# A fused dynamic convolution, LayerNorm and MLP on one core: W1 on SyncE's queue behind the first x, the first columns and their halo in one transfer, the first convolution chunk summed without VectorE, and a new order

## The chip, the cores and the metric

The kernel runs on one core of a Trainium2 chip. The metric is the device time of one execution in microseconds; the number that counts is the median of several runs.

## The reference

x has 8 batches of 4224 tokens of 192 channels, `weight_gen` has for each token 8 heads of 7 raw weights. What is computed, cut to its core:

```
w   = exp(weight_gen - max) / sum                # softmax over the 7 taps
y   = sum over k of w[.., k] * x[s - 6 + k]      # causal, 24 channels share a head's weight
xn  = (y - mean) / sqrt(var + 1e-6) * g          # over the 192 channels
out = y + relu(xn @ w1) @ w2                     # w1 192x768, w2 768x192, given as float64
```

## The kernel before

**Layout.** The 33792 tokens lie over the 128 partitions, 16 stretches of each of the 8 batches, so a partition owns C = 264 consecutive tokens, called columns. The convolution of a column reaches 6 columns back. Those of a stretch's first columns belong to the partition ahead (the halo); the first stretch of each batch has zeros there, written by a memset. x passes through a ring `X` of 36 columns with 6 halo columns ahead of it.

**Loops.** The columns are cut three ways: softmax parts (`SOFT`: 4, 8, then 12 columns), norm parts and convolution chunks. The norm parts are

```
PARTS = (4,) * 6 + (8,) * 6 + (12,) * 15 + (8, 4)
```

and a convolution chunk has at most 6 columns (4 at the start). TensorE works in 66 groups g0 to g65 of 4 columns, that is 512 tokens each; a 12-column part feeds three of them.

**The work of a chunk.** VectorE multiplies x by the weights for taps two at a time (L383, three products `pr` of two taps and one `y`). GpSimd issues two DMAs that add one half of a `pr` to its other half (L389), and then adds four `pr` halves into `y` (L386). For chunk 0 alone (`c < EARLY`, EARLY = 1) it is otherwise: one GpSimd addition of two whole `pr` (L399) and four additions by VectorE (L386). ScalarE then takes sums (L427) and squares (L432) of `y`, and a reciprocal root by logarithm and exponential (L455 to L457); VectorE refines it by a Newton step (L460 to L466); ScalarE writes the normalised `xh` (L478) and casts it to f16 `hl` (L485); GpSimd writes the low f16 part (L487); SyncE's queue moves it through a transposing DMA into `xT` (L491; two `hl` and three `xT` buffers).

**TensorE.** A group has three steps u0, u1, u2 of the first product (L506, 10 matmuls 128x512 each into `ph`). After each, ScalarE takes the relu into `hh` (L515), and VectorE the f16 remainder `hlo` (L517). The second product (L538 to L540) has four pieces of 18 matmuls, one for each column of a group; two of them stand between one step and another, so that they use `hh` and `hlo` of the group ahead. VectorE scales and adds it to `y` (L551), and a DMA takes `y` out (L558).

**Weights.** W1 and W2 come as pairs of 32-bit words. VectorE turns W1's words into f32 (L610 to L620, two row blocks of 128 and 64 rows, tiles `hh` for the words, `ph` and `hlo`), ScalarE takes sums of squares (L623), TensorE sums them over partitions (L630 and the matmul of L639, the first two matmuls of the program), VectorE makes a scale `c_gi` of them (L675), ScalarE scales W1 into `c_w1h` and keeps the scaled f32 (L680), GpSimd forms `c_w1l` (L683), and small DMAs shift row blocks (L686). W2 follows in the same way while the first groups run. W1's words are loaded by two DMAs on ScalarE's queue (L580), ahead of the two tiny loads of g. The loads of x (L287 halo, L290 and L292), of `weight_gen` (L298) and of W2 (L580) are on SyncE's queue.

**The order.** Nothing is scheduled by hand. Each operation is recorded with an engine, a cost and a due position `want`, in columns, which is the column that it works for less a number out of `WANT`, `W_WANT` or `FIRST`. `Plan.order` then places operations one by one on modelled engines: the earliest due of those that could start within `AHEAD` of the earliest, and that are due within `WINDOW` of the oldest operation left. The order so found is the program order of every engine's queue, and each engine keeps to it, waiting where an input or a buffer isn't ready.

Of the kernel before, what the change touches and what calls it, by code (L numbers as in the profile page):

```python
# [16 lines left out]
P = 128  # L17
# [2 lines left out]

PARTS = (4,) * 6 + (8,) * 6 + (12,) * 15 + (8, 4)
SOFT = (4, 8) + (12,) * 21
EARLY = 1
CHUNK = 6
RING = 36
HALF = 512
TINY = struct.unpack("<f", struct.pack("<I", (1023 - 126) << 20))[0]


WANT = {'load': 35.31, 'wload': 45.13, 'max': 23.73, 'sub': 26.8, 'exp': 29.21, 'sum': 19.41,  # L30
    'rcp': 16.76, 'inv': 19.08, 'mul': 14.75, 'conv': 17.87, 'step': 0.85, 'dma': -0.4, 'add':
    0.2, 'sums': 8.31, 'squares': 3.24, 'rstd': 5.29, 'newton': 6.27, 'xh': 1.75, 'lo': 6.1}
W_WANT = {'load': 23.7, 'a': 23.19, 'c': 24.61, 's1': 21.01, 'load2': 14.54, 'c2': 3.68, 's2':
    7.55}
FIRST = {'soft': -1.12, 'conv': -1.17, 'norm': 7.8}
AHEAD = 13.38
WINDOW = 11.37


class Buf:  # L40
# [11 lines left out]
class Plan:  # L52


    DMA_START = {"SP": 1250.0, "Pool": 650.0, "ACT": 1250.0}
    DMA_END = 1000.0

    def __init__(self):
# [30 lines left out]
    def order(self):  # L89
# [31 lines left out]
        while len(out) < len(self.ops):  # L121
            pick = None
            while by_want[lead].start is not None:
                lead += 1
            until = by_want[lead].want + WINDOW
            for e, c in cand.items():
                rows = [(t, o) for t, o in ((earliest(o), o) for o in c if o.want <= until)
                        if t is not None]
                if rows:
                    t0 = min(t for t, _ in rows) + AHEAD  # L130
                    row = min((r for r in rows if r[0] <= t0), key=lambda r: (r[1].want, r[1].rank))
# [25 lines left out]
def kernel(  # L157
# [10 lines left out]
    B, S, D = x.shape  # L168
# [3 lines left out]
    w1b, w2b = w1.bitcast(I32), w2.bitcast(I32)  # L172
    F = w1.shape[1]
    PAD = K - 1
    NF = F // P
    NB = 3
    C = B * S // P
    PB = P // B
# [4 lines left out]
    V, A, Q, T_, SY = nc.vector, nc.scalar, nc.gpsimd, nc.tensor, nc.sync  # L183
# [9 lines left out]
    X = cp.tile([P, PAD + RING, D], F32, name="x")  # L193
# [36 lines left out]
    def dma_ns(n):  # L230
        return n * P / 280.0
# [11 lines left out]
    xf = x.rearrange("b s d -> (b s) d")  # L243
# [26 lines left out]
    def xcol(t):  # L270

        return PAD + t % RING

    def xkey(t, back=False):
        return ("x", "h") if back else ("x", t % RING)

    def sp(want, fn, r, w, dma):
        op("SP", 450, want, fn, r=r, w=w, dma=dma)

    def load_x(ch):  # L280
        t0, n = ch["S"], ch["n"]
        want = t0 - WANT["load"]
        if t0 == 0:

            def first():
                src = bass.AP(tensor=xf.tensor, offset=(C - PAD) * D, ap=[[C * D, PB - 1], [PB * C * D, B], [1, PAD * D]])
                SY.dma_start(X[B:P, 0:PAD, :].rearrange("p t d -> p (t d)"), src)  # L287
            sp(want, first, [], [("x", "h")], dma_ns(PAD * D))
        elif t0 % RING == 0:
            sp(want, lambda: SY.dma_start(X[:, 0:PAD, :].rearrange("p t d -> p (t d)"), tokens(x, t0 - PAD, PAD)), [], [("x", "h")],  # L290
               dma_ns(PAD * D * 4))
        sp(want, lambda: SY.dma_start(X[:, xcol(t0) : xcol(t0) + n, :].rearrange("p t d -> p (t d)"), tokens(x, t0, n)), [],  # L292
           [xkey(t) for t in range(t0, t0 + n)], dma_ns(n * D * 4))

    def load_w(pa):
        t0, n = pa["S"], pa["n"]
        wb = pa["w"] = Buf("w")
        sp(t0 - WANT["wload"], lambda: SY.dma_start(at(wb)[:, :n, :].rearrange("p t f -> p (t f)"), tokens(wf, t0, n)), [], [wb],  # L298
           dma_ns(n * HK * 4))

    def early(s, what):
        return s - FIRST[what] * max(0.0, 1 - s / 12)

    def softmax(pa):
# [12 lines left out]
        def step(eng, cost, name, fn, r, w):  # L317
            op(eng, cost, S0 - WANT[name], fn, r, w)

# [31 lines left out]
    def conv(c):  # L351
        ch = chunks[c]
        t0, n, o = ch["S"], ch["n"], ch["so"]
        st = WANT["step"] * n / 6
        c0 = early(t0, "conv") - WANT["conv"]
        y = ch["y"] = Buf("y")
        prs = {k: Buf("pr") for k in (1, 3, 5)}
        wrap = t0 % RING == 0
        base = 0 if wrap else xcol(t0) - PAD
        xr = [xkey(t) for t in range(t0, t0 + n)]  # L360
        if wrap:
            xr.append(("x", "h"))
        else:
            xr += [xkey(t) for t in range(max(t0 - PAD, t0 // RING * RING), t0)]
            if t0 % RING < PAD:
                xr.append(("x", "h"))
        yw = [(y, j) for j in range(n)]

        def flat(k):
            if k == 0:  # L370
                return at(y)[:, :n, :].rearrange("p t d -> p (t d)")
            return at(prs[(k - 1) // 2 * 2 + 1])[:, (k - 1) % 2, :n, :].rearrange("p t d -> p (t d)")

        def mul(k, nk):
            wv = (WN[:, o * HK : (o + n) * HK].rearrange("p (m k) -> p k m", k=K)[:, k : k + nk, :]
                  .unsqueeze(3).broadcast_to([P, nk, n * H, G]))
            a = X[:, base + k : base + k + n, :]
            xv = bass.AP(tensor=a.tensor, offset=a.offset, ap=[a.ap[0], [D, nk], [G, n * H], [1, G]])
            if k:
                ov = at(prs[k])[:, :, :n, :].rearrange("p k t (h g) -> p k (t h) g", g=G)  # L380
            else:
                ov = at(y)[:, :n, :].rearrange("p t (h g) -> p (t h) g", g=G).unsqueeze(1)
            V.tensor_tensor(out=ov, in0=xv, in1=wv, op=ALU.mult)  # L383

        def add(k, E=Q):
            E.tensor_tensor(out=flat(0), in0=flat(0), in1=flat(k), op=ALU.add)  # L386

        def dma_add(to, k):
            Q.dma_start(flat(to), flat(k), accum_op=ALU.add, max_dma_last_dim=CHUNK * D * 4)  # L389

        nd = n * D
        for i, k in enumerate((1, 3, 0, 5)):
            op("V", v_ns(2 * nd if k else nd), c0 + 2 * i * st, lambda k=k: mul(k, 2 if k else 1),
               [*xr, "wn"], [(prs[k], 0), (prs[k], 1)] if k else yw)
        if c < EARLY:

            both = [(prs[k], h) for k in (1, 3) for h in (0, 1)]
            pp2 = [at_pair(prs[k], n) for k in (1, 3)]
            op("Pool", q_ns(2 * nd), c0, lambda: Q.tensor_tensor(out=pp2[0](), in0=pp2[0](), in1=pp2[1](), op=ALU.add),  # L399
               both[2:], both[:2])  # L400
            for i, (k, h) in enumerate(((5, 0), (5, 1), (1, 0), (1, 1))):
                op("V", v_ns(nd), c0 + (8 + i) * st, lambda k=k, h=h: add(k + h, V), [(prs[k], h)], yw)
            return
        for i, k in enumerate((1, 3)):
            op("Pool", 900, c0 + 2 * i * st + WANT["dma"], lambda k=k: dma_add(k, k + 1), [(prs[k], 1)],
               [(prs[k], 0)], dma=3300.0 * n / 6)
        for i, (k, h) in enumerate(((5, 0), (5, 1), (1, 0), (3, 0))):
            op("Pool", q_ns(nd), c0 + (4 + 2 * i) * st + WANT["add"], lambda k=k, h=h: add(k + h),
               [(prs[k], h)], yw)
# [161 lines left out]
    top, bot = slice(0, 64), slice(64, P)  # L571
    raw = (Buf("hh"), Buf("hh"), Buf("pr"))

    def words(i, o, n):
        return at(raw[i]).bitcast(I32).rearrange("p a b d -> p (a b d)" if i == 2 else "p j q -> p (j q)")[:, o : o + n]

    def load_weights():

        def dma(eng, E, want, dst, src, n, w):
            op(eng, 450, -W_WANT[want], lambda: E.dma_start(dst(), src), w=[w], dma=dma_ns(n))  # L580

        dma("ACT", A, "load", lambda: words(0, 0, 2 * F), w1b[0:P, :], 8 * F, raw[0])
        dma("ACT", A, "load", lambda: words(1, 0, 2 * F)[top, :], w1b[P:D, :], 4 * F, raw[1])
        dma("ACT", A, "load", lambda: W["g"][:, 0:1], gcol[0:P, :], 200, "g0")
        dma("ACT", A, "load", lambda: W["g"][top, 1:2], gcol[P:D, :], 100, "g1")
        wv2 = w2b.rearrange("(j p) d -> p j d", p=P)
        dma("SP", SY, "load2", lambda: words(2, 0, 2 * NF * D).rearrange("p (j d) -> p j d", d=2 * D), wv2,
            8 * NF * D, raw[2])

    def from_double(want, src, dst, n, sq, r, w, space="ph", rows=slice(0, P)):  # L590
# [14 lines left out]

        want = -W_WANT[want]
        op("ACT", a_ns(n), want, lambda: A.activation(mv(), part(1).bitcast(F32), AF.Square), r, [m])
# [17 lines left out]
    def w_scale(want, ss, bound, rt, r, w):  # L625


        pb = Buf("po")
        want = -W_WANT[want]
        op("PE", 240, want, lambda: T_.matmul(at(pb)[:, 0:1], ones, ss, start=True, stop=True), r, [pb],  # L630
# [18 lines left out]
    def weights():  # L649
# [5 lines left out]
        def f32(b, n, o=0):  # L655
            if b is not w2r:
# [5 lines left out]
                    [raw[1]], [wc], rows=top)  # L662
        want = -W_WANT["s1"]

# [35 lines left out]
        for h in range(3):  # L700
            from_double("c2", lambda h=h: words(2, 2 * h * tn, 2 * tn), lambda h=h: f32(w2r, tn, h * tn),
                        tn, s2[:, h : h + 1], [raw[2]], [(w2r, h)], "po")
        want2 = -W_WANT["s2"]
        op("V", 70, want2, lambda: V.tensor_reduce(out=s2[:, 3:4], in_=s2[:, 0:3], axis=AX.X, op=ALU.add),
# [69 lines left out]
```

## Time and profile before

| | |
|---|---|
| runs | 911.36, 912.03, 919.35 us; median 912.03 us |
| profiled execution | 914.2 us, of which the span of the trace is 912.4 us |
| busy in the span | TensorE 831.8 us (91%), VectorE 788.4 (86%), GpSimd 689.9 (76%), ScalarE 667.1 (73%) |
| first matmul of g0 | 57.65 us after the span's start |
| last matmul | starts at 907.39 us |

Times below are microseconds from the start of the span. A row of the timeline has start, duration, engine, line, operation, tiles, and in brackets the idle time of the engine ahead of it and what ended it. PE is TensorE, DVE VectorE, ACT ScalarE, POOL GpSimd, SP SyncE; SPq, ACTq and POOLq are their queues, where a DMA is issued. The row of a DMA in the timeline is its issue; when its data has landed comes from another view, which gives the time from issue to landing.

### The profile page before, as it was taken

What the parts mean: (1) busy time and instruction counts of PE and PEld (TensorE: products, weight loads), DVE (VectorE), ACT (ScalarE), POOL (GpSimd) and SP (SyncE); (2) the same over time, 40 slices, a digit from 0 to 9 for tenths busy, and PEclk for the clock granted to TensorE, in tenths of its full rate; (3) what the DMA queues carried; (4) which work ended last, traced back from release to release, by engine and by line L of the source; (5) the groups of instructions that cost most, each with busy time, mean ns of one, the idle gap of its engine ahead of it and who ended that gap; (6) DMA issues with size and microseconds to landing.
All of it is one profiled execution on the core that took longest, in us unless ns stands there. A gap on an engine that the chain in (4) does not pass through costs nothing. (4 is left out here: it accounts for less than half of the span.)

```text
span 912.4 us, 17537 instructions
## 1 busy us (share of the span) xinstructions
PE 831.8 (91%) x6736; PEld 587.2 (64%) x6736; DVE 788.4 (86%) x837; ACT 667.1 (73%) x1766; POOL 689.9 (76%) x398
## 2 busy tenths in 40 slices
PE   0029899999999999999999999999999999999997
PEld 0015577666767677776666667777677777677776
DVE  4999899999999999889798898998989989884342
ACT  1488778897779779787686878878788787787421
POOL 2499999999988898797776978878788787793100
PEclk9998999999999999999999999999999999999999
DMA  9587998889997899989979899798998997965311
GB/s 229 157 178 155 142 195 180 192 180 116 201 222 165 186 149 169 200 146 197 148 154 179 147 205 157 171 201 136 203 163 156 190 151 145 140 111 91 75 30 52
DMA packets 138667, 145.12 MB, mean 159 GB/s; under 512 B 107551, under 2 KB 108831, under 8 KB 138583
## 3 DMA queue, kind: packets, MB, share of 16 engines
q1 hardware_dynamic: 123735, 91.70, 51.4%
q0 software_dynamic: 14400, 51.12, 32.6%
q10 hardware_dynamic: 448, 1.18, 0.5%
q8 instruction: 52, 0.85, 0.4%
q14 instruction: 32, 0.26, 0.1%
HBM read 40.56 MB, written 25.95 MB: 73 GB/s over the span
## 5 line engine op out<-in xcount | busy, mean ns | idle before, releaser
L386 POOL TENSOR_TENSOR y<-y,pr 128x1152 f32<-128x1152 f32 (+1 forms) x200 | 490.1, 2488 | 75.5 <-DVE pr L383 67.7
L506 PE MATMUL ph<-xT,c_w1h 128*128 128x512 f16 x1188 | 421.4, 383 | 43.1 <-DMA xT<-hl 33.5
L540 PE MATMUL po<-c_w2h,hlo 128*128 128x192 f16 x1584 | 389.8, 246 | 5.5 <-DVE hlo L517 5.4
L538 PE MATMUL po<-c_w2h,hh 128*128 128x192 f16 x1584 | 389.7, 246 | 0.0
L539 PE MATMUL po<-c_w2l,hh 128*128 128x192 f16 x1584 | 389.7, 246 | 0.0
L383 DVE TENSOR_TENSOR pr<-x,wn 128x2304 f32<-128x2304 f32 (+1 forms) x153 | 338.1, 2217 | 3.1
L517 DVE SCALAR_TENSOR_TENSOR hlo<-ph,hh 128x1024 f16<-128x1024 f32 x198 | 241.3, 1219 | 81.6 <-ACT hh L515 81.3
L506 PE MATMUL ph<-xT,c_w1l 128*128 128x512 f16 x792 | 303.2, 383 | 0.0
L515 ACT ACTIVATE hh<-ph 128x1024 f16<-128x1024 f32 x198 | 199.9, 1010 | 78.3 <-PE ph L506 77.2
L506 PEld LDWEIGHTS <-c_w1h 128*128 128x128 f16 x1188 | 117.2, 99 | 128.3 <-ACT c_w1h L680 6.3
L538 PEld LDWEIGHTS <-hh 128*128 128x128 f16 x1584 | 155.0, 98 | 22.7
L539 PEld LDWEIGHTS <-hh 128*128 128x128 f16 x1584 | 155.0, 98 | 22.7
L540 PEld LDWEIGHTS <-hlo 128*128 128x128 f16 x1584 | 155.0, 98 | 8.6 <-DVE hlo L517 8.0
L478 ACT ACTIVATE xh<-y,s 128x192 f32<-128x192 f32 x264 | 123.7, 535 | 39.6 <-DVE s L466 39.5
L487 POOL TENSOR_TENSOR hl<-xh,hl 128x768 f16<-128x768 f32 x66 | 118.3, 1792 | 40.7 <-ACT hl L485 39.6
L506 PEld LDWEIGHTS <-c_w1l 128*128 128x128 f16 x792 | 78.1, 99 | 110.2 <-POOL y L386 24.1
L427 ACT ACTIVATE junk<-y 128x192 f32<-128x192 f32 x264 | 95.2, 361 | 45.5 <-POOL y L386 36.0
L432 ACT ACTIVATE junk<-y,s 128x192 f32<-128x192 f32 x264 | 119.1, 451 | 6.0
L389 POOL DMA_DIRECT2D pr<-pr x100 | 100.0, 1003 | 20.7 <-DVE pr L383 19.8
L551 DVE SCALAR_TENSOR_TENSOR y<-po,c_fs,y 128x384 f32<-128x384 f32 x132 | 80.3, 608 | 12.7 <-PE po L540 12.7
L485 ACT ACTIVATE hl<-xh 128x768 f16<-128x768 f32 x66 | 55.1, 835 | 27.7 <-DMA xT<-hl 27.5
L383 DVE TENSOR_TENSOR y<-x,wn 128x1152 f32<-128x1152 f32 (+1 forms) x51 | 60.1, 1180 | 0.1
(63 smaller groups left out, 328.4 us busy)
## 6 DMA issues: line engine op xcount, KB each, us to landing
pr<-pr POOLq DMA_DIRECT2D x60, 576.0 KB, 9.7
x<-in_x_dram SPq DMA_DIRECT2D x37, 576.0 KB, 8.5
out_dram<-y SPq DMA_DIRECT2D x30, 576.0 KB, 7.2
pr<-pr POOLq DMA_DIRECT2D x40, 384.0 KB, 6.5
x<-in_x_dram SPq DMA_DIRECT2D x21, 384.0 KB, 7.9
out_dram<-y SPq DMA_DIRECT2D x21, 384.0 KB, 3.9
w<-in_weight_gen_dram SPq DMA_DIRECT2D x21, 336.0 KB, 8.6
pr<-in_moe_w_ch_dram SPq DMA_DIRECT2D x1, 1152.0 KB, 11.3
```

The lines of the kernel that those rows point to most:

```text
L383: V.tensor_tensor(out=ov, in0=xv, in1=wv, op=ALU.mult)
L386: E.tensor_tensor(out=flat(0), in0=flat(0), in1=flat(k), op=ALU.add)
L389: Q.dma_start(flat(to), flat(k), accum_op=ALU.add, max_dma_last_dim=CHUNK * D * 4)
L432: A.activation(junk, at(y)[:, j, :], AF.Square, bias=at(s4)[:, 3, t : t + 1], accum_out=at(s4)[:, 0, t : t + 1])
L478: A.activation(at(xh)[:, t, :], at(y)[:, i, :], AF.Identity, bias=at(s4)[:, 3, g + t : g + t + 1], scale=at(s4)[:, 1, g + t : g + t + 1])
L487: lambda xh=xh, hl=hl: Q.tensor_tensor(out=at(hl)[:, :, 1, :], in0=at(xh), in1=at(hl)[:, :, 0, :], op=ALU.subtract),
L506: T_.matmul(at(ph)[:, v, :], w[:, wb, fsl], xv[:, xb, :, :], start=(i == 0), stop=(i == len(steps) - 1))
L515: lambda us=us, ph=ph: A.activation(at(hh)[:, us, :], at(ph), AF.Relu), [ph], [(hh, u)])
L517: lambda us=us, ph=ph: V.scalar_tensor_tensor(out=at(hlo)[:, us, :], in0=at(ph), scalar=0.0, in1=at(hh)[:, us, :], op0=ALU.max, op1=ALU.su ...
L538: T_.matmul(o, at(hh)[:, j, q], w2h[:, j, :], start=(j == 0), stop=False)
L539: T_.matmul(o, at(hh)[:, j, q], w2l[:, j, :], start=False, stop=False)
L540: T_.matmul(o, at(hlo)[:, j, q], w2h[:, j, :], start=False, stop=(j == NF - 1))
```

## The change

Four things are changed, and lines after them move down by 7 to 9 (L383 becomes L392, L485 L494, L491 L500, L515 L524, L580 L589, L610 L619, L680 L689).

- The halo and the first four columns of x, 10 columns in all, come in one DMA of 120 partitions (900 KB); the first stretch of each batch, 8 partitions, gets its four columns by a DMA of its own (24 KB, key `("x","f")`). Before, these were 540 KB (halo) and 384 KB.
- W1's two loads (768 KB and 384 KB) are issued by SyncE, no longer by ScalarE.
- EARLY is 0: chunk 0 is summed as all others are, by two accumulating DMAs and four additions on GpSimd.
- All numbers of the planner are new, and its modelled start of a DMA on SyncE's queue is 900 ns, not 1250 ns. So the order changes everywhere.

```diff
-EARLY = 1
+EARLY = 0
...
-WANT = {'load': 35.31, 'wload': 45.13, 'max': 23.73, ... 'conv': 17.87, 'step': 0.85, 'dma': -0.4, 'add':
-    0.2, 'sums': 8.31, 'squares': 3.24, 'rstd': 5.29, 'newton': 6.27, 'xh': 1.75, 'lo': 6.1}
+WANT = {'load': 38.24, 'wload': 44.92, 'max': 23.79, ... 'conv': 16.93, 'step': 0.73, 'dma': -0.01, 'add':
+    -1.02, 'sums': 7.16, 'squares': 1.78, 'rstd': 3.89, 'newton': 7.22, 'xh': 6.49, 'lo': 6.25}
...
-    DMA_START = {"SP": 1250.0, "Pool": 650.0, "ACT": 1250.0}
+    DMA_START = {"SP": 900.0, "Pool": 650.0, "ACT": 1250.0}
...
             def first():
-                src = bass.AP(tensor=xf.tensor, offset=(C - PAD) * D, ap=[[C * D, PB - 1], [PB * C * D, B], [1, PAD * D]])
-                SY.dma_start(X[B:P, 0:PAD, :].rearrange("p t d -> p (t d)"), src)
-            sp(want, first, [], [("x", "h")], dma_ns(PAD * D))
-        elif t0 % RING == 0:
+                src = bass.AP(tensor=xf.tensor, offset=(C - PAD) * D,
+                              ap=[[C * D, PB - 1], [PB * C * D, B], [1, (PAD + n) * D]])
+                SY.dma_start(X[B:P, 0 : PAD + n, :].rearrange("p t d -> p (t d)"), src)
+
+            cols = [xkey(t) for t in range(n)]
+            sp(want, first, [], [("x", "h"), *cols], dma_ns((PAD + n) * D))
+            src = bass.AP(tensor=xf.tensor, offset=0, ap=[[PB * C * D, B], [1, n * D]])
+            sp(want, lambda: SY.dma_start(X[0:B, PAD : PAD + n, :].rearrange("p t d -> p (t d)"), src), [],
+               [("x", "f")], 300.0)
+            return
+        if t0 % RING == 0:
...
+        if t0 < RING:
+            xr.append(("x", "f"))
...
-        dma("ACT", A, "load", lambda: words(0, 0, 2 * F), w1b[0:P, :], 8 * F, raw[0])
-        dma("ACT", A, "load", lambda: words(1, 0, 2 * F)[top, :], w1b[P:D, :], 4 * F, raw[1])
+        dma("SP", SY, "load", lambda: words(0, 0, 2 * F), w1b[0:P, :], 8 * F, raw[0])
+        dma("SP", SY, "load", lambda: words(1, 0, 2 * F)[top, :], w1b[P:D, :], 4 * F, raw[1])
```

Three places show what this does to the order. A row is a line of the kernel, the operation, what it writes and reads, and the shape.

The first is SyncE's queue from its first DMA on. Before, it holds no load of W1:

```order
L298 DMA w_64<-in_weight_gen_dram 128x1x224
L298 DMA w_65<-in_weight_gen_dram 128x1x448
L287 DMA x<-in_x_dram 120x1x1152
L292 DMA x<-in_x_dram 128x1x768
L298 DMA w_66<-in_weight_gen_dram 128x1x672
L292 DMA x<-in_x_dram 128x1x768 x4
```

After:

```order
L305 DMA w_64<-in_weight_gen_dram 128x1x224
L305 DMA w_65<-in_weight_gen_dram 128x1x448
L288 DMA x<-in_x_dram 120x1x1920
L293 DMA x<-in_x_dram 8x768
L299 DMA x<-in_x_dram 128x1x768
L305 DMA w_66<-in_weight_gen_dram 128x1x672
L589 DMA hh_88<-in_moe_w_ch_dram 128x1536
L589 DMA hh_89<-in_moe_w_ch_dram 64x1536
```

W1 (`hh_88`, `hh_89`) now stands behind one further load of x and one of weights.

The second is VectorE from the first product on. Before, the words of W1 follow two of chunk 0's products, and its four additions (L386) stand among the scale of W1:

```order
L383 TENSOR_TENSOR pr_77<-x,wn_102 128x2x768
L383 TENSOR_TENSOR pr_78<-x,wn_102 128x2x768
L610 TENSOR_SCALAR ph_103<-hh_88 128x768
L610 TENSOR_SCALAR ph_104<-hh_89 64x768
...
L645 RECIPROCAL c_r_118<-c_r_118 128x1
L386 TENSOR_TENSOR y_67<-y_67,pr_78 128x768
L675 TENSOR_SCALAR c_gi<-c_g,c_r_118 128x2
L386 TENSOR_TENSOR y_67<-y_67,pr_78 128x768
L344 TENSOR_TENSOR wn_102<-e_97,wn_102 128x448
L386 TENSOR_TENSOR y_67<-y_67,pr_77 128x768
```

After:

```order
L392 TENSOR_TENSOR pr_76<-x,wn_102 128x2x768
L392 TENSOR_TENSOR pr_77<-x,wn_102 128x2x768
L335 TENSOR_REDUCE wn_102<-e_97 128x64
L392 TENSOR_TENSOR y_67<-x,wn_102 128x768
L619 TENSOR_SCALAR ph_103<-hh_88 128x768
L392 TENSOR_TENSOR pr_79<-x,wn_102 128x2x768
L619 TENSOR_SCALAR ph_104<-hh_89 64x768
...
L654 RECIPROCAL c_r_118<-c_r_118 128x1
L392 TENSOR_TENSOR y_68<-x,wn_102 128x768
L684 TENSOR_SCALAR c_gi<-c_g,c_r_118 128x2
```

Three of chunk 0's four products stand ahead of the first use of W1 (L619), and the last of them right behind it; no addition of `y` is left on VectorE.

The third is ScalarE in the steady part, around the cast (L485) of g36, the first group of a 12-column part. Before, the cast stands between the relu (L515) of g34's u1 and that of its u2:

```order
L457 ACTIVATE s_98<-s_98 128x12
L515 ACTIVATE hh_88<-ph_103 128x1024
L478 ACTIVATE xh_81<-y_70,s_98 128x192 x4
L478 ACTIVATE xh_82<-y_70,s_98 128x192 x2
L515 ACTIVATE hh_88<-ph_104 128x1024
L326 ACTIVATE e_97<-e_97 128x672
L485 ACTIVATE hl_83<-xh_81 128x4x192
```

After, the first relu below is that of g34's u1 and the second that of its u2:

```order
L524 ACTIVATE hh_88<-ph_104 128x1024
L333 ACTIVATE e_97<-e_97 128x672
L464 ACTIVATE s_98<-s_98,bias 128x12
L465 ACTIVATE s_98<-s_98 128x12
L466 ACTIVATE s_98<-s_98 128x12
L524 ACTIVATE hh_88<-ph_103 128x1024
L487 ACTIVATE xh_81<-y_70,s_98 128x192 x4
L487 ACTIVATE xh_82<-y_70,s_98 128x192 x2
L494 ACTIVATE hl_83<-xh_81 128x4x192
```

The root, the normalisation and the cast have moved behind one relu more. Of the 15 parts of 12 columns, eleven are changed in this way, by one relu; in the other four the cast (that of g18, g27, g39 and g48) now stands behind the relu of u0 of the group just ahead of its own, a step later still.

More of the change, by code (lines that the diff above doesn't have):

```diff
@@ L27 @@
 TINY = struct.unpack("<f", struct.pack("<I", (1023 - 126) << 20))[0]
-WANT = {'load': 35.31, 'wload': 45.13, 'max': 23.73, 'sub': 26.8, 'exp': 29.21, 'sum': 19.41,
-    'rcp': 16.76, 'inv': 19.08, 'mul': 14.75, 'conv': 17.87, 'step': 0.85, 'dma': -0.4, 'add':
-    0.2, 'sums': 8.31, 'squares': 3.24, 'rstd': 5.29, 'newton': 6.27, 'xh': 1.75, 'lo': 6.1}
[L33 to L37, printed above, removed]
+WANT = {'load': 38.24, 'wload': 44.92, 'max': 23.79, 'sub': 26.54, 'exp': 28.86, 'sum': 21.12,
+    'rcp': 16.07, 'inv': 16.09, 'mul': 20.37, 'conv': 16.93, 'step': 0.73, 'dma': -0.01, 'add':
+    -1.02, 'sums': 7.16, 'squares': 1.78, 'rstd': 3.89, 'newton': 7.22, 'xh': 6.49, 'lo': 6.25}
+W_WANT = {'load': 31.07, 'a': 23.29, 'c': 26.27, 's1': 17.43, 'load2': 14.58, 'c2': 15.87, 's2':
+    7.16}
+FIRST = {'soft': 4.72, 'conv': 4.6, 'norm': 5.98}
+AHEAD = 17.1
+WINDOW = 11.68
 class Buf:
```

## The prediction

> **What bounds the kernel now.** I read the page's first two parts, then what TensorE waits for, the stretch from the fifth group to the end, and the chain.
>
> ```profile
> PE 831.8 (91%) x6736; PEld 587.2 (64%) x6736; DVE 788.4 (86%) x837; ACT 667.1 (73%) x1766; POOL 689.9 (76%) x398
> ...
> PE   0029899999999999999999999999999999999997
> ```
> ```profile
> PE ph L506 <- DMA xT<-hl: 33.5, 4, 30.4
> PE po L630 <- DVE c_s L670: 26.6, 1, 26.6
> PE ph L506 <- DVE hlo L517: 9.3, 10, 4.6
> ```
> ```profile
> 118.00:907.00 789.00, 779.47 (x6393) 1.00 0.86 158
> ```
> ```profile
> 818.27 2.16 PE ph L506 x10
> ...
> 830.69 2.16 PE ph L506 x10
> ```
>
> In the slices TensorE is idle for the first two and full after the fourth. Its waits (us in total, times, the longest) say the same: 26.6 + 30.4 us go by before the first group, and little later. From 118.00 us on (columns: length, TensorE busy with its matmuls, granted clock, DMA share, GB/s) it is busy 779.47 us of 789.00. There it works at a fixed pace, since the same step of two groups that follow each other starts 830.69 - 818.27 = 12.42 us apart. So there are three things to price: when the first groups come, what is lost later, and whether the new order loses more.
>
> ```profile
> 57.65 0.59 PE L506 MATMUL ph<-xT,c_w1h 128*128 128x512 f16 x1 [30.43 <-DMA xT<-hl]
> 69.33 0.59 PE L506 MATMUL ph<-xT,c_w1h 128*128 128x512 f16 x1 [4.58 <-DVE hlo L517]
> 118.00 0.39 PE L506 MATMUL ph<-xT,c_w1h 128*128 128x512 f16 x1 [0.46 <-DMA xT<-hl]
> ```
> ```profile
> 14.29:98.91 84.62, 36.53 (x230) 21.95 (x231) 81.83 (x117) 56.32 (x157) 64.11 (x43) 0.96 0.77 169
> ```
>
> The rows at 57.65 and 118.00 are the starts of g0 and g4, both waiting for their transposes, and the one at 69.33 is g0's u2. The second view has columns for PE, PEld, DVE, ACT and POOL: from chunk 0's first product (14.29) to the Newton step for g4 (98.91) VectorE is busy 81.83 us of 84.62. **Up to g4 VectorE sets the time, and after it TensorE.** Between 118.00 and the last matmul at 907.39 lie 789.4 us, against 61 groups at 12.42 and the last with its tail of 18.4 us, 776 in all: 13.4 us are lost later, a little at a time.
>
> **The change: x and W1.**
>
> ```profile
> 0.77 0.96 ACTq L580 DMA_DIRECT2D hh<-in_moe_w_ch_dram  x2
> 2.11 1.02 SPq L287 DMA_DIRECT2D x<-in_x_dram  x1
> 3.18 0.61 SPq L292 DMA_DIRECT2D x<-in_x_dram  x1
> ...
> 6.12 0.39 DVE L321 TENSOR_REDUCE mx<-w 128x32 f32<-128x224 f32 x1 [5.07 <-DMA w<-in_weight_gen_dram]
> ...
> 11.89 0.39 ACT L326 ACTIVATE e<-e 128x224 f32<-128x224 f32 x1 [9.87 <-DMA x<-in_x_dram]
> 14.29 3.42 DVE L383 TENSOR_TENSOR pr<-x,wn 128x1536 f32<-128x1536 f32 x2
> 17.63 1.80 DVE L610 TENSOR_SCALAR ph<-hh 128x768 int32<-128x768 int32 x2
> 22.80 1.80 DVE L620 SCALAR_TENSOR_TENSOR hlo<-pr,ph 128x768 f32<-128x768 f32 x2
> ```
> ```profile
> hh<-in_moe_w_ch_dram ACTq DMA_DIRECT2D x1, 768.0 KB, 4.6
> x<-in_x_dram SPq DMA_DIRECT2D x1, 540.0 KB, 9.2
> ```
> ```profile
> x<-in_x_dram SPq DMA_DIRECT2D x1, 384.0 KB, 9.8
> ```
>
> From issue to landing W1's first part takes 4.6 us, so it is there at 5.4; the halo comes at 2.11 + 9.2 = 11.3, the first x at 3.18 + 9.8 = 13.0. The last 384 KB came in 1.7 us, 230 KB/us. Moving W1's 1152 KB behind x lets x come earlier by 1152/230 = 5.0 us at most, at 8.0. The other bound is the softmax: its exponential ran at 11.89 only because ScalarE stood in its own queue's DMA issues until then, and from it to the first product are 14.29 - 11.89 = 2.4 us; without that it could run at about 7.2 (the weights are there at 6.12, then 1.1 us of maximum and subtraction, as its row and the subtraction's 0.58 in the trace add up with their gaps), which gives 9.6. I take 8.7 between them: the first product **5.6 us earlier**.
>
> W1 then lands behind 24 + 384 KB of x and 336 KB of weights, 744/230 = 3.2 us, and its 768 KB take 3.3 us at that rate or, since the 4.6 us above hold the latency of a transfer too, as little as 2: 13.9 to 15.2 alone. Chunk 0's two accumulating DMAs, issued at about 10.5 and 12.2, run beside it: up to 19. I take 16.3. VectorE reaches the first use of W1 after 3.42 us of products, 0.6 of sum and 0.95 of `y`, at 13.65. It **waits 2.65 us** there, and everything behind it on VectorE waits too.
>
> The trace prices the merge itself only by its bytes. The Trainium skill (DMA: Bandwidth & Descriptors, "Why a DMA increments its semaphore by 16 and not by 1") has a rule that speaks against it: a transfer is spread over the largest number of engines up to 16 that divides its slowest dimensions, so the 120 partitions, whose source has 15 outer rows, would go over 15 and the 8 partitions over 8. The halo had those 15 rows before; by the rule the 360 KB that join it would take 16/15 of 1.6 us and the 24 KB twice 0.1, together 0.2 more (an estimate), and the sum below would be 3.1 instead of 3.3. No row here shows the engines of a transfer.
>
> **The change: chunk 0's additions.**
>
> ```profile
> L386 DVE TENSOR_TENSOR y<-y,pr 128x768 f32<-128x768 f32 x4 | 4.8, 1195 | 0.0
> ```
> ```profile
> L386 POOL TENSOR_TENSOR y<-y,pr 128x768 f32<-128x768 f32 x8 | 15.1, 1886 | 2.0 <-DVE pr L383 1.7
> ```
> ```profile
> 32.22 0.22 DVE L675 TENSOR_SCALAR c_gi<-c_g,c_r 128x2 f32<-128x2 f32 x1
> 34.13 1.75 ACT L680 ACTIVATE hlo<-hlo,c_gi 128x768 f32<-128x768 f32 x2
> ...
> 39.79 0.36 ACT L427 ACTIVATE junk<-y 128x192 f32<-128x192 f32 x1 [3.25 <-DVE y L386]
> ...
> 52.02 2.37 SPq L491 DMA_TRANSPOSE xT<-hl  x1
> ```
> ```profile
> xT<-hl SPq DMA_TRANSPOSE x1, 5.6
> ```
>
> VectorE loses four additions, 4.8 us (one was drawn out to about twice the others: I count 3.7). GpSimd gains four at 1.9 us and two DMA issues and loses one addition; with its products early and the exponential's subtraction between, `y` of chunk 0 is whole at about 32.5, where it was at 39.75. What is late next is W1's scale. From 16.3 VectorE has its eight operations on W1 (17.63 to 24.60 in the trace, 7.0), one product between them (1.75), then two products, one of `y` and 3.2 of small work: 16.3 + 7.0 + 1.75 + 3.5 + 0.95 + 3.2 = 32.7 for `c_gi`, against 32.4 before. So **ScalarE's scaling of W1 ends at 36.1** (3.4 us behind `c_gi`, as the row at 34.13 ends 3.4 behind the one at 32.22), and the sums of g0, which waited for `y` until 39.79, start then, 3.7 us sooner. From there to the transposes the trace has 52.02 - 39.79 = 12.2 us, and 5.6 more to their landing: g0 starts at **53.9 instead of 57.65** (51.5 to 56.5 by the bounds on W1).
>
> **What reaches g4.** VectorE starts 5.6 us sooner and loses 3.7. Against that stand the wait for W1 (2.65), 0.7 us of other rows that the new order places ahead of g4's Newton step, and waits on relu steps of the first groups, which VectorE now reaches before TensorE has delivered: the row at 69.33 shows how these two wait for each other there. In the new order g0's first piece of the second product stands ahead of g1's u0, so such a wait comes earlier; I take 2.7, half way between none and the 4.58 of the row at 69.33 with a little more for a second one. The sum: 5.6 + 3.7 - 2.65 - 0.7 - 2.7 = **3.3 us earlier at g4**. With W1 in time it is 5.9, with W1 at 19.1 it is 0.5.
>
> **The steady part.** The third piece of order is the one that I cannot call free.
>
> ```profile
> 507.35 2.74 ACT L478 ACTIVATE xh<-y,s 128x192 f32<-128x192 f32 x6 [2.59 <-DVE s L466]
> ...
> 511.55 0.83 ACT L485 ACTIVATE hl<-xh 128x768 f16<-128x768 f32 x1
> ...
> 512.58 1.94 POOL L487 TENSOR_TENSOR hl<-xh,hl 128x768 f16<-128x768 f32 x1
> 513.16 1.00 ACT L515 ACTIVATE hh<-ph 128x1024 f16<-128x1024 f32 x1
> ...
> 514.17 1.18 POOL L389 DMA_DIRECT2D pr<-pr  x1
> 514.54 1.43 SPq L491 DMA_TRANSPOSE xT<-hl  x1
> ```
> ```profile
> 513.79 0.38 PE L506 MATMUL ph<-xT,c_w1h 128*128 128x512 f16 x1
> ```
> ```profile
> xT<-hl SPq DMA_TRANSPOSE x1, 10.6
> ```
> ```profile
> DMA to landing us min/median/max: 3.2/8.1/15.4
> ```
>
> g35 starts at T = 513.79, and g36 at T + 12.4. Its transposes are issued at T + 0.75 and land 10.6 us later, only 1.1 us ahead of need; they run beside an accumulating DMA issued 0.4 us ahead. In the changed order the six normalisations, the cast and the low part come behind the relu of g34's u2. That relu can end at T - 1.6 (between u2 and T stand two of the four pieces of the second product, half of 12.42 - 3 x 2.16, so u2 ends 3.0 before T, and the relu takes 1.0) or, as in the trace, at T + 0.4. Then 2.74 + 0.83 + 1.94 us pass, and the transposes are issued at T + 3.9 to T + 5.9. At the median of all transposes, 8.1, they land between 0.4 us in time and 1.6 late; at 10.6, 2.1 to 4.1 late; at the least, 3.2, in time. What speaks for the shorter ones: for g36 the accumulating DMA now stands one addition of GpSimd ahead of the low part, no longer behind it. I therefore price this at nothing in the forecast, leave the 13.4 us of later losses as they are, and give the late case a large chance.
>
> **The sum.** 914.2 - 3.3 = 910.9 for the profiled execution. That was 2.2 us above the median of 912.03, so the median comes to about **909 us**.
>
> **The rivals.** *The cast is late in every part.* One mechanism with one place, the first transposes of each 12-column part; it decides as soon as they take over 8.5 us from issue (T + 12.4 less T + 3.9), and at about 1 us for each of 15 parts it costs 15 us: 914.2 - 3.3 + 15 - 2.2 = 924; at 10.6 us for all it would be 15 x 3 = 45, or 954. For it: the 10.6 of the row above. Against: the collision that made it moves away. *W1 in time, and smoother later*: the head gives 5.9, and half of the 13.4 lost later goes, since VectorE comes to each step of the second product with more lead (9.3 us of TensorE's waits were for `hlo`): 914.2 - 5.9 - 6.7 - 2.2 = 899.4. For it: after g4 no engine is full but TensorE. Against: two accumulating DMAs run beside W1. *The change doesn't do what it says*: W1 lands at 19 or later, the head gives 0.5, 912.
>
> **How the numbers follow.** Forecast 0.47 (909, its own range 904 to 916); late cast 0.24 (924, 917 and up); in time and smoother 0.22 (900, 895 to 905); nothing gained 0.07 (912). 1%, about what a measurement of this kernel can tell from no change, is 902.9 to 921.2. Faster: three quarters of the third case and a little of the first, 0.19. Slower: four fifths of the second and a little of the first, 0.22. The rest, 0.59, is within. The range 898 to 927 leaves out 0.07 below and 0.09 above.
>
> **What would show it.** In the profile after: chunk 0's first product at 8.7 and a wait of VectorE for a DMA of W1 of 2.65 us (right behind the first product of `y`); `c_gi` near 32.7; g0 at 53.9; g4 at 114.7; no additions on VectorE. Waits of TensorE for `xT` once in each 12-column part, in all over 8 us, would show the late cast. A last stretch from g4 of much less than 789 us would show the third case. The forecast is wrong if W1 lands after 19, if the pace in the steady part is no longer 12.42, or if VectorE waits for the first groups by more than the 2.7 that I took.

## The result, and the profile after

| | before | after |
|---|---|---|
| median of the runs | 912.34 us | 918.58 us |
| ratio after to before | | 1.0071 (95% interval 1.0049 to 1.0094) |
| a second set, on one chip | 909.94 | 918.63, ratio 1.0098 (1.0066 to 1.0130) |
| span of the profile used here | 912.4 | 913.1 |

The change makes the kernel 0.7 to 1.0% slower. The profile below is from the second set, since the one of the first set fell into a disturbed execution, with a span of 929.6 us. The execution profiled here is the quickest of its set, and the profile before is of one at 914.2 us, above its median, so most of the 6 us is not in the comparison.

The head, first. The rows are of VectorE's first product, its first use of W1, `c_gi` and the end of the Newton step for g4, and of TensorE's first matmul of g0 and of g4:

```profile
10.52 3.42 DVE L392 TENSOR_TENSOR pr<-x,wn 128x1536 f32<-128x1536 f32 x2 [3.07 <-DMA x<-in_x_dram]
16.30 0.96 DVE L619 TENSOR_SCALAR ph<-hh 128x768 int32<-128x768 int32 x1 [0.65 <-DMA hh<-in_moe_w_ch_dram]
34.19 0.35 DVE L684 TENSOR_SCALAR c_gi<-c_g,c_r 128x2 f32<-128x2 f32 x1
94.83 0.15 DVE L475 TENSOR_TENSOR s<-wn,s 128x4 f32<-128x4 f32 x1
```
```profile
54.97 0.58 PE L515 MATMUL ph<-xT,c_w1h 128*128 128x512 f16 x1 [3.44 <-DMA xT<-hl]
...
108.60 0.38 PE L515 MATMUL ph<-xT,c_w1h 128*128 128x512 f16 x1
```

g4 starts at 108.60 where it was 118.00: the head gains 9.4 us. Then the rest in three stretches (g4 to g14, g14 to g18, g18 to the end), after and, in the second fence, before; the columns are the stretch, its length, TensorE's busy time, the granted clock, the DMA share and GB/s:

```profile
108.60:236.04 127.44, 124.82 (x1024) 1.00 0.87 182
236.04:299.87 63.83, 54.27 (x411) 0.92 1.09 158
299.87:907.40 607.53, 603.25 (x4961) 1.00 0.72 151
```
```profile
118.00:243.95 125.95, 124.91 (x1020) 1.00 0.90 177
243.95:297.31 53.36, 50.31 (x410) 1.00 0.95 192
297.31:907.40 610.09, 604.64 (x4970) 1.00 0.84 151
```

Four groups, g14 to g17, take 63.83 us instead of 53.36. So 9.4 won at the head, 1.5 lost up to g14, **10.5 lost in four groups**, and 1.8 won from g18 to the start of g65. Against the pace of 12.42 us for a group these four lose 14.1 us; in the profile of the first set they lose 31.3, while from g18 to g65 the two agree (589.8 and 589.9 us), so it is the length of this stretch that differs between the two executions. What lies in it is seen in the issues of DMAs around g15's transposes and in the view of landings (the time from issue to landing is the last number):

```profile
229.09 0.59 SPq L299 DMA_DIRECT2D x<-in_x_dram  x1
229.78 4.82 SPq L500 DMA_TRANSPOSE xT<-hl  x1
```
```profile
230.30 1.71 POOL L398 DMA_DIRECT2D pr<-pr  x2
```
```profile
xT<-hl SPq DMA_TRANSPOSE x1, 20.3
```
```profile
234.00:238.00 4.00, 4.00 (x37) 1.00 1.45 85
238.00:242.00 4.00, 4.00 (x32) 1.00 1.45 35
```
```profile
250.10 0.39 PE L515 MATMUL ph<-xT,c_w1h 128*128 128x512 f16 x1 [0.51 <-DMA xT<-hl]
```

A load of x, the transposes of g15 and two accumulating DMAs are issued within 1.8 us. The transposes take 20.3 us; in between the DMA engines count as busy (1.45; the share adds up the times of all packets that start in the stretch, so it can pass 1) and move 35 to 85 GB/s, where the stretch as a whole had 158. TensorE itself waits only 0.51 us for the landing at 250.05. Most of its waiting comes by way of the accumulating DMAs, which land 20 and 23 us after their issue:

```profile
250.38 2.61 POOL L395 TENSOR_TENSOR y<-y,pr 128x1152 f32<-128x1152 f32 x1 [9.66 <-DMA pr<-pr]
257.21 0.36 ACT L436 ACTIVATE junk<-y 128x192 f32<-128x192 f32 x1 [5.38 <-POOL y L395]
263.48 0.58 PE L515 MATMUL ph<-xT,c_w1h 128*128 128x512 f16 x1 [5.92 <-DVE hlo L526]
```
```profile
263.48:270.70 7.22, 7.22 (x46) 0.70 1.19 105
```

GpSimd's addition waits 9.66 us for such a DMA, ScalarE's sums wait for the addition, the relu that TensorE needs next stands behind those sums in ScalarE's program order, VectorE waits for the relu to form `hlo`, and TensorE waits 5.92 us for that. In the whole stretch TensorE waits 8.8 us for `hlo`, where it was 2.7 before. Of the 10.5 us lost, 6.5 are more waiting, nearly all of it this; the other 4.0 are the matmuls themselves, which keep TensorE busy for 54.27 us instead of 50.31 for the same work: the granted clock over the stretch is 0.92 instead of 1.00, and 0.70 in the 7.22 us right behind the long wait. A second long landing is that of g17's transposes, 23.9 us.

### The profile page after: what moved, and what is told of

It is laid out like the page before. It is cut to its first block, busy times and chain, and to the rows that moved or that the text cites. A ratio compares the mean times of both kernels' runs of the same rounds, so it can differ in the third digit from the quotient of the medians.

```text
span 929.6 us, 17536 instructions
## 1 busy us (share of the span) xinstructions
PE 833.0 (90%) x6736; PEld 588.3 (63%) x6736; DVE 785.3 (84%) x833; ACT 669.6 (72%) x1766; POOL 694.8 (75%) x403
## 3 DMA queue, kind: packets, MB, share of 16 engines
q0 software_dynamic: 14688, 51.91, 31.3%
## 5 line engine op out<-in xcount | busy, mean ns | idle before, releaser
L395 POOL TENSOR_TENSOR y<-y,pr 128x1152 f32<-128x1152 f32 (+1 forms) x204 | 505.1, 2501 | 109.5 <-DVE pr L392 75.9
L515 PE MATMUL ph<-xT,c_w1h 128*128 128x512 f16 x1188 | 422.1, 384 | 40.3 <-DVE hlo L526 28.7
L392 DVE TENSOR_TENSOR pr<-x,wn 128x2304 f32<-128x2304 f32 (+1 forms) x153 | 337.7, 2217 | 5.3 <-DMA x<-in_x_dram 3.3
L515 PE MATMUL ph<-xT,c_w1l 128*128 128x512 f16 x792 | 303.8, 384 | 0.0
L524 ACT ACTIVATE hh<-ph 128x1024 f16<-128x1024 f32 x198 | 200.1, 1011 | 104.6 <-PE ph L515 92.6
L515 PEld LDWEIGHTS <-c_w1h 128*128 128x128 f16 x1188 | 117.3, 99 | 129.4 <-DMA xT<-hl 8.5
L515 PEld LDWEIGHTS <-c_w1l 128*128 128x128 f16 x792 | 78.0, 99 | 108.5 <-issue 38.6
L496 POOL TENSOR_TENSOR hl<-xh,hl 128x768 f16<-128x768 f32 x66 | 114.6, 1756 | 40.0 <-ACT hl L494 38.7
L398 POOL DMA_DIRECT2D pr<-pr x102 | 105.7, 1060 | 18.9 <-DVE pr L392 15.7
L494 ACT ACTIVATE hl<-xh 128x768 f16<-128x768 f32 x66 | 55.1, 834 | 13.1 <-DMA xT<-hl 12.8
L392 DVE TENSOR_TENSOR y<-x,wn 128x1152 f32<-128x1152 f32 (+1 forms) x51 | 60.2, 1182 | 0.3
```

What stands on the lines that cost most here:

```text
L496: lambda xh=xh, hl=hl: Q.tensor_tensor(out=at(hl)[:, :, 1, :], in0=at(xh), in1=at(hl)[:, :, 0, :], op=ALU.subtract),
L515: T_.matmul(at(ph)[:, v, :], w[:, wb, fsl], xv[:, xb, :, :], start=(i == 0), stop=(i == len(steps) - 1))
L524: lambda us=us, ph=ph: A.activation(at(hh)[:, us, :], at(ph), AF.Relu), [ph], [(hh, u)])
```

## The experiments

**The same kernel again**, for the profile above.

> The changed kernel as it is, for a second profile. Theory: the head's gain is real (g0 near 54, g4 10 us earlier than before), and what loses it are one or two stretches between 200 and 320 us in which a transposing DMA and two accumulating DMAs are issued within 1 us of one another and all land some 25 us later: TensorE loses 10 to 16 us per stretch, at g14 to g17. Rival: the loss is spread over many groups, a little in each part, and the stretch in the first profile was an accident; then this profile has no group that loses over 4 us between g4 and g65. Time 914 to 920 by both.

Measured: 918.63 us. g14 to g17 lose 14.1 us in all (63.83 less 4 x 12.42), no other group above 3.4; the loss is in one place. In two further kernels that keep the order of this place (the split and W1 runs below) it is 19.5 and 14.8 us.

**The change in two halves: structure and numbers.** Either the changed program with the old planner numbers, or the old program with the new ones:

```diff
-WANT = {'load': 38.24, 'wload': 44.92, ...
+WANT = {'load': 35.31, 'wload': 45.13, ...
```

> The changed program (W1 on SyncE's queue, merged first load, no additions by VectorE) with the planner's numbers of before. If the loss comes from the new numbers alone, this keeps most of the head's gain and is faster than before: 902 to 908. If W1 behind x or chunk 0's sums on GpSimd cost the time, it is slower than before, 915 or more.

> The kernel before with the planner's new numbers, and nothing else changed. If the new numbers place the colliding transfers, it has a stretch in which transposes take over 20 us as in the changed kernel, and takes 915 to 930. If the changed structure causes the collisions, it stays near 912 or below.

Measured: structure alone 922.92, ratio 1.0161 (1.0121 to 1.0201); numbers alone 914.62, 1.0058 (1.0043 to 1.0073). Neither half is good by itself. With the structure alone the first product is early, but g4 starts at 121.06, and its 12-column parts keep the long transposes of before (11.3 us at g39):

```profile
121.06 0.38 PE L515 MATMUL ph<-xT,c_w1h 128*128 128x512 f16 x1 [0.54 <-DVE hlo L526]
```
```profile
pr<-pr POOLq DMA_DIRECT2D x1, 576.0 KB, 10.9
xT<-hl SPq DMA_TRANSPOSE x1, 11.3
```

It also has a long stretch of its own, the transposes of g12 and g13 (14.0 and 19.0 us), by which TensorE loses 8.8 us in g11 and g12. With the numbers alone the long transposes of the 12-column parts go; g15's and g17's take 9.5 and 9.2, not 20, and it is the head that is lost: g1's transposes are issued only at 79.86. So neither half has the stretch at g15 and g17: it needs the order that both make together. The numbers alone did not place it, as one branch had it, and yet the time is above the 912 of the other branch.

```profile
79.86 1.43 SPq L491 DMA_TRANSPOSE xT<-hl  x1
```

**The kernel before, with an accumulating DMA moved away from each low part.** The order is kept; after the planning one rule moves DMAs on GpSimd's queue:

```diff
+    """Moves an accumulating DMA that GpSimd issues next to a low part behind up to two of its next operations."""
...
-    for o in plan.order():
+    for o in keep_apart(plan.order()):
         o.fn()
```

> The kernel before, its order as it is except that an accumulating DMA which stands next to a low part on GpSimd is issued up to two operations (2 to 5 us) later. If transposes and an accumulating DMA that start together slow each other, the transposes of the first group of each 12-column part fall from 10 to 13 us to below 7 and TensorE's late losses of 13 us shrink by at least half: 904 to 908. If the transposes are long for another reason (two of them close together, or the load of x), they stay above 9 us and the time stays within 911 to 914, or rises since the sums wait.

Measured: 904.03 us, ratio 0.9943 (0.9927 to 0.9960). The transposes of the first groups of the 12-column parts, 8.3 to 13.9 us before, take 3.2 to 4.8; over all groups:

```profile
DMA to landing us min/median/max: 3.2/3.7/11.6
```
```profile
116.78:878.60 761.82, 758.88 (x6223) 1.00 0.79 163
```

From g4 to the start of g65 (the row stops 0.1 us ahead of it) TensorE now needs 761.9 us, where it needed 771.0 before: of the 13.4 us that I took for order, about 9 were this meeting of an accumulating DMA with the transposes. That is the difference of two profiled executions, and the one before was at 914.2 us; the medians of the runs differ by 5.9 us in all.

**The changed kernel with the same kind of rule**, in a weak form (a DMA followed by another DMA stays) and a strong one (two other operations must lie between a low part and an accumulating DMA).

> The same with a weaker rule: a DMA within two operations behind a low part moves, except where another DMA follows it. So g17's and g31's neighbours move, g15's pair stays as it is. By the theory g15 keeps its 20 us and g17 falls below 10: about half of the gain, 904 to 912. If the moved DMAs work by something else (a later sum, another load on VectorE), g15 changes as well, or neither does.

> The changed kernel, its order kept, but an accumulating DMA is held on GpSimd until two other operations stand between a low part and it; this moves the pair behind g15's low part and the one right behind g17's and g31's. If the transfers that start together are the cause, the transposes of g15 and g17 land within 10 us (they took 20 and 24), TensorE loses under 4 us from g14 to g17 (it lost 14), and the time is 897 to 905. If a stretch of slow transfers comes there whatever starts with what, the transposes stay near 20 us and the time near 918.

Measured: weak 920.74, ratio 1.0123 (1.0101 to 1.0144); strong 908.86, 0.9983 (0.9968 to 0.9998). The rules tell the groups apart as expected: with the weak one g17's transposes are short and g15's, whose pair stays, take 28.4; with the strong one both are short and the stretch from g14 to g18 takes 53.14 us.

```profile
pr<-pr POOLq DMA_DIRECT2D x1, 576.0 KB, 28.6
xT<-hl SPq DMA_TRANSPOSE x1, 28.4
```
```profile
242.41:295.55 53.14, 50.32 (x412) 1.00 0.89 191
```

But both times missed the range. Both rules also hold back a DMA behind g0's low part, and the head pays for that: g4 starts at 113.83 and 115.00 instead of 108.60. With the weak rule g15's stretch is longer too: g14 to g17 lose 17.6 us there, not about half of the 14. So the strong rule was tried **from g13 on alone**:

> The changed kernel with the stronger rule (two other operations of GpSimd between a low part and an accumulating DMA) from g13's low part on alone, so that the head's order is untouched. By the theory the head keeps g4 near 108.6, g14 to g17 lose under 4 us, and the time is the changed kernel's 918 (a profile of 913 span) less 10 to 13: 900 to 906, faster than before. If the head's gain and the collision hang together (what comes early at the head must be waited for at g15), the loss only moves, and the time stays above 910.

Measured: 902.72 us, ratio 0.9915 (0.9899 to 0.9932), faster than both kernels. g4 starts at 107.66, and g14 to g17 take 0.8 us less than before the change:

```profile
235.06:287.66 52.60, 50.31 (x411) 1.00 0.88 190
```
```profile
DMA to landing us min/median/max: 3.2/3.7/8.8
```

**What the meeting needs.** First collisions put in on purpose in the version just above, and plain copies in place of the accumulating ones in the changed kernel, which leaves half of the products out of the sum:

```diff
+def collide(out, dose={36: 2, 45: 1}):
+    """Puts the last one or two accumulating DMAs ahead of a low part right behind it."""
...
-            Q.dma_start(flat(to), flat(k), accum_op=ALU.add, max_dma_last_dim=CHUNK * D * 4)
+            Q.dma_start(flat(to), flat(k), max_dma_last_dim=CHUNK * D * 4)
```

> The version just above, with collisions put in on purpose: behind g36's low part two accumulating DMAs, behind g45's low part one, where both had stood ahead of it. By the theory the transposes of g36 take 20 us or more and those of g45 10 to 14 (they took 3.2 to 3.4), all others of the 12-column parts stay under 9, and TensorE loses 8 to 14 us near g36 and under 3 near g45. If the slow stretch at g15 was due to its place in the program, neither changes by more than 3 us.

> The changed kernel with its order, but the accumulating DMAs are plain copies of the same size on the same queue (so half of the taps' products are left out of the sum). If it is the accumulation (read, add, write) that makes the shared stretch slow, the transposes of g15 and g17 fall below 12 us; if any large transfer from GpSimd's queue that starts with a transpose does it, they stay near 20.

Measured: in the first, 7.7 us at g36 and 9.1 at g45 (one run, 907.99), so two accumulating DMAs are not enough for a stretch of 20 us, and my account was incomplete. With plain copies (one run, 900.59) g15's transposes still take 18.0 and g17's 9.7; at g15 it needn't be an accumulation. TensorE loses only 1.6 us in g14 to g17 all the same, so transposes of 18 us alone don't make the loss. What was ahead of g15's and g17's transposes in their own queue, and not of g36's, was a load of x. So four mixtures in one kernel, and the loads of x put behind the transposes in the changed one:

```diff
+    """g24: the next load of x right ahead of its transposes. g33: that, and two accumulating DMAs right behind the low
+    part. g39: the two DMAs alone. g45: the load and one DMA."""
...
+def x_behind(out, groups=(15, 17)):
+    """Puts the loads of x that stand ahead of a group's transposes, behind the transposes before, behind them."""
```

> The kernel with the DMAs held back from g13 on, and in four 12-column parts a mixture put in on purpose at the first transposes: g24 a load of x (576 KB) issued right ahead of them, g33 that and two accumulating DMAs right behind the low part, g39 the two DMAs alone, g45 the load and one DMA. If the long stretches need all three kinds at once (transposes, a load ahead of them in their own queue, accumulating DMAs beside them), g33 lands after 15 us or more, g45 after 10 to 14, g24 and g39 below 9. If the number of accumulating DMAs alone sets it, g33 and g39 are alike. If it takes none of these, all stay below 9.

> The changed kernel with its order, the accumulating DMAs where they are, but the loads of x that stand ahead of the transposes of g15 and g17 on SyncE's queue are issued behind them. If the load ahead is needed for the long stretch, both groups' transposes fall from 20 to 25 us below 12, and the time to 903 to 910. If the accumulating DMAs are enough, they stay at 20 and the time at 918.

Measured in the first (one run, 920.7 us), from issue to landing of the transposes of g24 (load alone), g33 (load and two DMAs), g39 (two DMAs alone) and g45 (load and one DMA):

```profile
xT<-hl SPq DMA_TRANSPOSE x1, 6.1
```
```profile
xT<-hl SPq DMA_TRANSPOSE x1, 15.4
```
```profile
xT<-hl SPq DMA_TRANSPOSE x1, 7.6
```
```profile
xT<-hl SPq DMA_TRANSPOSE x1, 7.6
```
```profile
479.00:483.00 4.00, 0.00 (x0) 0.92 1.73 94
```

Of these four only the mixture of all three is long, and in it the DMA share again goes far above 1 at a low rate (last row: TensorE idle, share 1.73, 94 GB/s). One accumulating DMA with a load did no more here than two without, 7.6 us and not the 10 to 14 expected. Each mixture was tried at one place, and the DMAs were not issued at the same distance from the transposes, so this is not yet a rule; the last section has cases that do not fit it. In the second kernel all accumulating DMAs stay where they were; with the loads of x behind, g15's transposes take 7.7 us, TensorE loses under 2 us in g14 to g17, and the time is 903.59, ratio 0.9916 (0.9888 to 0.9944). So at g15 it takes both: without the DMAs beside them (the version from g13) the transposes take 6.2 us, without the load ahead 7.7, with both 20.3.

**The last long stretch**, g32's transposes (25.4 us in the changed kernel), with the load of x put behind these as well:

> The changed kernel with the loads of x behind the transposes of g15, g17 and now g32 too, where the last long stretch is (28 us, TensorE loses 6 near g31 and g32). If a load ahead is needed for it, g32's transposes fall below 15 and the time by 3 to 6 to 898 to 901; if not, the time stays at 903.6.

Measured: 902.11, ratio 0.9892 (0.9860 to 0.9923). The transposes take 17.0 us, still long, so the load ahead isn't all of it here; but they are there in time, and g31 and g32 lose nothing where they lost 5.9 in the run just above. Against 903.59 the difference is within the spread of the runs.

**The parts of the head.** W1's loads given back to ScalarE's queue, the first load split again (in the changed kernel, and in the version with the rule from g13), all with the order kept; and EARLY = 1, where the order shifts with it.

```diff
-        dma("SP", SY, "load", lambda: words(0, 0, 2 * F), w1b[0:P, :], 8 * F, raw[0])
+        dma("SP", A, "load", lambda: words(0, 0, 2 * F), w1b[0:P, :], 8 * F, raw[0])
...
-                              ap=[[C * D, PB - 1], [PB * C * D, B], [1, (PAD + n) * D]])
+                              ap=[[C * D, PB - 1], [PB * C * D, B], [1, PAD * D]])
...
-EARLY = 0
+EARLY = 1
```

> The changed kernel with its order, but W1's two loads are issued by ScalarE again, behind the loads of g. My theory of the head: W1 behind x gives VectorE's first product about 4 us; so here the first product comes at 11 to 14 us, W1 by 9, and g4 is 2 to 5 us later than with W1 on SyncE's queue (108.6). Rival: W1's queue does not matter, since what the first product gains VectorE waits for again at W1; then g4 stays within 1 us of 108.6.

> The changed kernel with its order, but the halo (540 KB) and the first four columns (384 KB) are two transfers again. If the merge matters for itself, the first product comes over 0.5 us later than in the changed kernel; if only the bytes count, within 0.5 us, and g4 within 1 us of 108.6.

> The version of the first run with the first load split again into halo and first columns. The split alone brought the first product from 10.5 to 8.6 us, and g4 from 108.6 to 107.7. If g4 hangs on the first product, this is 1 to 2 us faster than the merged version; if the wait for W1 takes it up, both agree within 1 us.

> The changed kernel with EARLY = 1 again (chunk 0 by one GpSimd addition and four of VectorE), the planner's new numbers kept, so the order shifts with it. If taking the additions from VectorE is worth their 3.7 us, the Newton step for g4 ends 2 to 6 us later than the 95.0 of the changed kernel and g4 starts later than 108.6 by as much. If they were hidden, both stay within 1 us.

Measured: the first product of the W1 run and that of the split run (both VectorE), and the start of g4 with W1 on ScalarE's queue, split, and with EARLY = 1 (TensorE, one run each):

```profile
15.16 1.75 DVE L392 TENSOR_TENSOR pr<-x,wn 128x1536 f32<-128x1536 f32 x1 [7.45 <-DMA x<-in_x_dram]
```
```profile
8.59 1.75 DVE L391 TENSOR_TENSOR pr<-x,wn 128x1536 f32<-128x1536 f32 x1 [1.13 <-DMA x<-in_x_dram]
```
```profile
113.11 0.38 PE L515 MATMUL ph<-xT,c_w1h 128*128 128x512 f16 x1
```
```profile
107.74 0.38 PE L514 MATMUL ph<-xT,c_w1h 128*128 128x512 f16 x1
```
```profile
111.63 0.38 PE L515 MATMUL ph<-xT,c_w1h 128*128 128x512 f16 x1
```

The W1 and split runs took 929.06 and 918.03 us; both keep the long stretches. Seven profiles whose order is that of the changed kernel up to g4 have g4 at 107.48 to 110.08, so these differences are to be read against that spread. W1 behind x is worth 4.5 us at g4 (3.0 to 5.6); its first product came later than the 11 to 14 expected. Taking the additions from VectorE is worth 3.0 (1.5 to 4.2; the last part of the Newton step for g4 starts at 97.14 instead of 94.83), as far as a run can tell whose order has shifted as well. The merge costs the first product 1.9 us, which neither branch of the expectation had: it comes at 9.75 to 10.75 in all profiles with the merged load and W1 behind it, and at 8.59 and 8.34 in the two with the split. How much of this reaches g4 can't be told from the spread (107.74 and 107.28 with the split), since most of it goes into the wait for W1; with the rule from g13 the split is no faster that can be told (901.93 against 902.72, ratios 0.9912 and 0.9915). The run with EARLY = 1 took 901.79 us, although its head is 3 us worse: in its order the two accumulating DMAs are issued 1.6 and 2.2 us behind g15's transposes, not 0.5 and 1.1, and these take 9.3 us.

## Why the prediction was wrong

The forecast was 0.3% faster, and the kernel is 0.7% slower; its time lies inside the range, but the sign is wrong. That it lies inside is partly luck: in the profiles the head gave 6.1 us more than forecast, and the part behind it lost 10.1 us more, 23.5 instead of the 13.4 that were carried over.

- **The head: mechanism right, one term mis-sized.** W1 was used at 16.30, as forecast (16.3), though by two errors that cancel: the first product came at 10.52 and not at 8.7, and the wait was 0.65, not 2.65. The term at fault is the merged load; with its halves apart, the first product is at 8.59, within 0.1 of the estimate, which went by bytes alone. That agreement is itself partly luck: 8.7 was set between two bounds that both had to be met, and the later of them, 9.6 for the softmax, was too late, since after the change the weights were ready at 7.45. The Trainium skill's rule that a transfer whose slowest dimension has 15 rows goes over 15 engines (DMA: Bandwidth & Descriptors, "Why a DMA increments its semaphore by 16 and not by 1") pointed the right way; the cost worked out from it was 0.2, the measured one is 1.9, and what makes up the difference is open. No row here shows which engines a transfer used. `c_gi` came at 34.19 (32.7 forecast), g0 at 54.97 (53.9), the Newton step for g4 ended at 94.98, 3.9 us sooner than before (3.3 forecast).
- **From that step to g4** the prediction carried over the time of before, and this is its first false step. Before, g4's transposes took 11.1 us with an accumulating DMA issued 0.74 us behind them, after 3.6 with one 1.14 us behind, both with a load of x some 1.6 to 1.9 us ahead; and g4 started at 108.60 rather than 114.7. The head gave 9.4, not 3.3 (7.9 to 10.5 by the seven profiles, against the one before).

```profile
xT<-hl SPq DMA_TRANSPOSE x1, 11.1
```
```profile
xT<-hl SPq DMA_TRANSPOSE x1, 3.6
```

- **The steady part** is where the sign was lost, and this is the step that failed: "leave the 13.4 us of later losses as they are", with the new order priced at nothing. They were not the small change of an order, but mostly one cause (9 us of them between the two profiles, by the kernel before with its DMAs apart), and a new order moves that cause about. In the 12-column parts it mostly went (g36's transposes took 3.3 us, though g32's took 25.4); in the 8-column parts it came back in a worse form, 14.1 us in four groups here and up to 19.5 in kernels that keep this place, where a load of x, the transposes and two accumulating DMAs are issued together. With the DMAs moved away (from g13 on), or with the loads moved away, the kernel is 0.8% faster than before the change.
- **The late cast** did not happen: g36's transposes were issued 5.6 us behind the start of g35, inside the 3.9 to 5.9 forecast, and landed 3.5 us ahead of need. I had the row that mattered, transposes of 10.6 us beside an accumulating DMA issued 0.4 us ahead, and saw that the order parts the two at g36. I asked what this does for g36 and didn't go through the other places where the order brings transfers together; the order of the two queues would have shown g15 and g17.
- **No rival** had this mechanism. The slower one named also had DMA landings that come too late, but at another place, by another cause, and through the transposes; here the loss came mostly through the accumulating DMAs and the engines that wait for them.

## What to carry to other kernels

Where the DMA engines are busy most of the time (from g4 on a share of 0.86 before the change and 0.78 after), a new order moves transfers against one another, and that can outweigh what the order was changed for. Look in the order for the places where a transpose, a large load in its queue and transfers of another queue are issued within a microsecond or two, and price these first. Issuing the loads of x behind the transposes of two groups was worth more here (15 us, from 918.6 to 903.6) than the whole replanned head (9 us).

## What the runs showed of the hardware

Transfers that start together can be far slower than one after another. In the places tried, a group's transposes took 3.2 us alone, 6.1 with a load of 576 KB issued right ahead of them, 7.6 to 7.7 with two accumulating DMAs beside them, 15.4 with both put together on purpose, and 20 to 28 at g15 in the changed kernel and those that keep its order there. The engines are counted busy all the while, at 35 to 94 GB/s.

What decides it is open. At g15 it isn't the accumulation alone, since plain copies gave 18.0 (and 9.7 at g17). The number of kinds isn't a rule either: before the change one accumulating DMA, issued 0.3 to 0.4 us ahead, went with transposes of 10.9 and 9.9 us at g57 and g60, where no load of x was under way; and at g17 after the change 23.9 us came with loads of x 1.6 and 2.3 us ahead and one such DMA issued with the transposes. A difference of a microsecond or less seems to matter. With the same load ahead at g15, the two DMAs came 0.5 and 1.1 us behind the transposes (20.3 us), 0.3 and 0.9 behind (26.8), 0.2 ahead and 0.4 behind (26.1 and 28.4), and 1.6 and 2.2 behind (9.3 and 9.5); these are different kernels, one profile each.

TensorE's granted clock was 0.70 in the 7.2 us behind a wait of 5.9 us at g15, and 1.00 in the same groups of the kernels without the long stretch.
